# Passing the first four blocks of a gated feed-forward network in two halves of its inner columns, and splitting half of its weights later

## Chip, core and metric

The kernel runs on one core of a Trainium2 chip. The metric is device time in microseconds (us) of one execution. The engines are named as the profile names them: PE is TensorE (PEld its weight load), DVE is VectorE, ACT is ScalarE, POOL is GpSimd, SP is SyncE, which issues most DMAs.

## The reference

All values are float32. Three stages follow one another on the same 3072 tokens (4 batches of 768) of width 320.

```python
# 1 recurrence: 4 x 8 heads, 768 steps, state 40 x 40
y[t] = r[t] @ state
state = state*w[t] - outer(state @ a[t], b[t]) + outer(v[t], k[t])
# 2 eight experts, one per token (D = 320, F = 1024)
logits = x @ w_gate + modality_bias[modality_id];  e = argmax(logits)
out[e_idx==e] = softmax(logits)[e] * (relu(x[e_idx==e] @ w1[e]) @ w2[e])
# 3 gated network, 3072 tokens (D = 320, inner F = 1536)
g = x @ w_gate2;  out = (silu(g) * (x @ w_val)) @ w_out
```

## The kernel before

The recurrence fills the first 570 us and is not touched. What follows is one function, `main`, whose instructions are issued in the order in which the code is written; every engine takes its own in that order.

**Precision.** A float32 matrix is used as two parts, a rounded one ("h") and the remainder ("l"); a product is three matmuls, h·h, l·h and h·l (`mm3`, L607 to L610). The last 64 of the 320 rows carry h and l in one tile, so a column of 128 inner units takes eight matmuls (`up`). An activation is split where it arises: ACT writes the rounded part, DVE the remainder.

**Experts.** The tokens, sorted by expert, fill eight static slots: seven of 384 tokens, slot 1 of 512. Each slot takes four steps `p` of 256 inner columns: up-matmuls, ReLU and split (`evac`, tile `hl`, L926), down-matmuls (tile `pd`). Each step also splits the next weights: ACT casts (L663), POOL subtracts (L664), two POOL instructions a step. The results go to a buffer `y1` in DRAM.

**Second network's weights.** Its three matrices come as the float64 numbers of the input, and are made into h and l parts on the chip by 22 chunks of eight operations each (`split64`, L566 to L576), eight on DVE with two beside them on ACT. That is 176 operations, taken one by one from a generator. A chunk is (gate, c), (value, c) of 192 inner columns or (out, c) of 256 inner rows, c rising. `prepare` takes them during slots 1 to 7 at an even rate: 150 of 176 by the last expert step, the rest in the first block of the second network.

**Second network.** The tokens pass in nine blocks, of 2, 3, 3, 3, 3, 3, 3, 2 and 2 tiles of 128. A block takes twelve columns `fc` of 128 inner units: up for gate and for value, silu on ACT (L1075), product on DVE (L1077, here "mul"), cast on ACT (L1080), remainder on DVE (L1081), and the down-matmuls one column later (`down2`). After column 11 the sums are copied to `ys` (L1058) and stored or scattered by POOL (L1059). The tokens of the next block are gathered by POOL from `y1` at column 0 (`xload`, L962), their gates at column 4 (`gates`, L967 and L968), multiplied on DVE at columns 7 to 9 (`gmul`, L972), and transposed on PE and split at columns 8 to 10 (`xt2`, L647, L622 to L624).

Buffers that matter: `pu` for the up-products has two, gate and value of one column; `pd` has four of one tile; `xg` has four; the split tokens `X` have two sets, for even and odd blocks.

Of the kernel before, what the change touches and what calls it, by code (L numbers as in the profile page):

```python
# [492 lines left out]
Q = {'SK': 8.0, 'TL': 11.0, 'RP': 12, 'ORD': '1dD2bBx', 'F2': (0, 4, 7), 'RS': [1, 4, 5, 3, 0, 3, 1, 2, 0, 0, 0, 0, 0, 0, 0, 0, 0, 0, 0, 0, 0, 0, 0, 0], 'G6': 0, 'HV': 1, 'DP': (1,), 'NV': 1, 'V1': (3,), 'V2': (2,)}  # L493
# [117 lines left out]
def up(T,out,w,x,fs,between=None):  # L611


    wh,wl=w; xh,xl=x
# [3 lines left out]
    T.matmul(out,wh[:,2,fs],xh[:,2],start=False,stop=False)  # L618
    T.matmul(out,wl[:,2,fs],xh[:,2],start=False,stop=True)  # L619
def xsplit(nc,ps,xh,xl,ts):  # L620
    V,A=nc.vector,nc.scalar
    A.copy(xh[:,0:2,ts],ps[:,0:2]); A.copy(xh[0:64,2,ts],ps[0:64,2])  # L622
    V.tensor_tensor(xl[:,0:2,ts],ps[:,0:2],xh[:,0:2,ts].bitcast(F32),ALU.subtract)
    V.tensor_tensor(xh[64:128,2,ts],ps[0:64,2],xh[0:64,2,ts].bitcast(F32),ALU.subtract)  # L624
class Moe:
# [13 lines left out]
    def xalloc(s, j):  # L639
        return tuple(s.xp.tile([128,3 if x=="xh" else 2,128*tiles(j%2)],F32R,tag=x+"eo"[j%2],name=x)[:,:,0:128*tiles(j)] for x in ("xh","xl"))  # L640
# [246 lines left out]
    def main(s, LG, y1, gd, wg, wv, wo, out):  # L887
        tc=s.tc; nc=s.nc; V,A,G,T=nc.vector,nc.scalar,nc.gpsimd,nc.tensor; C=s.C
        s.gd=gd
        with ExitStack() as ctx:  # L890
# [64 lines left out]
            XG={}; ID={}; GT={}  # L955
# [7 lines left out]
            def gates(b):  # L963
                if b>=len(blocks) or blocks[b][0]<0: return
                n=len(blocks[b])
                ID[b]=P.tile([128,NT,2],I32,tag="id",bufs=3,name="id"); GT[b]=P.tile([128,NT],F32,tag="gt",bufs=2,name="gt")
# [10 lines left out]
            def cut(x,n): return tuple(y[:,:,0:n] for y in x)  # L977
            def loop(n):
# [71 lines left out]
            def down2():  # L1050
                b,fc,hh,hl=pn; n=len(blocks[b])
                if fc==0: pds[b]=pdt(n)
                pd=pds[b]
                down(pd,fc==0,fc==11,hh,hl,W["o"][0][:,fc],W["o"][1][:,fc])
                if fc<11: return
                ys=ystile(); lastb=b==len(blocks)-1
# [110 lines left out]
```

## Time and profile before

| | us |
|---|---|
| median of 3 runs (1232.97 to 1238.61) | 1236.4 |
| profiled execution, its own time | 1238.5 |
| its span, first to last instruction | 1236.8 |
| PE busy over the span | 1073.2 (87%) |
| DVE busy | 853.8 (69%) |
| ACT, POOL busy | 557.7, 553.2 |
| mean granted TensorE clock | 0.938 |

The span has three parts: the recurrence to about 570 us, the experts to about 826 us, the second network to the end. A share over the whole span mixes them, so each part is read by itself.

### The profile page before, as it was taken

To read this page: it belongs to the slowest core of one execution; us is meant where nothing else is said; L and a number is where in the kernel's file an instruction comes from. 1 tells how busy PE (TensorE), PEld (TensorE's weight loads), DVE (VectorE), ACT (ScalarE), POOL (GpSimd) and SP (SyncE) were. 2 spreads that over 40 slices of the span, in tenths; PEclk is the share of its full clock that TensorE was granted. 3 is DMA by queue.
4 is the path that set the end of the run, shared out by engine and by line. 5 is a ranking of instruction groups with operands and counts; after the bars stand their busy time and mean duration, and the time that the engine had idled before them with its cause. 6 is when DMAs were issued, how large, how long until landed. Compare 5 with 4: busy or idle time off the path is not lost.

```text
span 1236.8 us, 27832 instructions
## 1 busy us (share of the span) xinstructions
PE 1073.2 (87%) x10437; PEld 1010.8 (82%) x10437; DVE 853.8 (69%) x1979; ACT 557.7 (45%) x1344; POOL 553.2 (45%) x1068
## 2 busy tenths in 40 slices
PE   5367888889889987987897787889999999999998
PEld 4356777778778877877787787889999999999998
DVE  5998898988888988645699999997233332333332
ACT  5355567566666664452354444443222222222232
POOL 7885676676656766221556556523111112111000
PEclk9677999999998899887998988899999999999999
DMA  6544446654555434312566566532000000000000
GB/s 108 88 78 86 79 74 114 118 118 87 99 105 98 79 78 87 83 47 73 157 185 177 164 186 185 156 106 72 17 22 21 18 17 23 28 11 28 11 17 12
DMA packets 278321, 102.39 MB, mean 83 GB/s; under 512 B 235713, under 2 KB 272961, under 8 KB 278177
## 3 DMA queue, kind: packets, MB, share of 16 engines
q1 hardware_dynamic: 270864, 85.56, 31.2%
q0 software_dynamic: 3856, 11.02, 3.0%
q10 hardware_dynamic: 3456, 3.93, 0.9%
q8 instruction: 86, 1.41, 0.5%
q14 instruction: 59, 0.48, 0.1%
HBM read 77.56 MB, written 22.90 MB: 81 GB/s over the span
## 4 chain that ended last, share of the span: by engine, by line
PE 36%; DVE 9%; issue 3%; DMA 1%; POOL 1%; ACT 1%; SPq 1%; DVEq 0%; POOLq 0%; ACTq 0%
PE pu L608 6%; PE pu L609 6%; PE pu L610 6%; PE pd L609 4%; PE pd L608 4%; PE pd L610 4%; PE pu L618 3%; PE pu L619 3%; DVE cva L575 1%; DVE cvm L569 1%; DVE hl L926 1%; DVE cva L567 1%; DVE cva L571 1%; DVE cva L568 1%; PE xt L647 1%
## 5 line engine op out<-in xcount | busy, mean ns | idle before, releaser
L1077 DVE TENSOR_TENSOR s<-s,pu 128x384 f32<-128x384 f32 (+1 forms) x108 | 55.0, 509 | 183.0 <-PE pu L619 180.3
L664 POOL TENSOR_TENSOR l<-s,h 128x768 fp32r<-128x768 f32 (+1 forms) x62 | 117.4, 1909 | 130.0 <-ACT h L663 118.4
L266 POOL TENSOR_TENSOR tmp<-Lb,Pm 128x60 f32<-128x60 f32 (+22 forms) x348 | 107.9, 310 | 54.3 <-DMA Lb<-LD 28.3
L266 DVE TENSOR_TENSOR tmp<-Lb,Pm 128x60 f32<-128x60 f32 (+24 forms) x372 | 112.0, 301 | 19.5 <-DMA Lb<-LD 8.3
L1080 ACT CAST hh<-s 128x384 fp32r<-128x384 f32 (+1 forms) x108 | 51.6, 478 | 146.9 <-DVE s L1077 146.8
L269 DVE TENSOR_TENSOR Pm<-Pm,tmp 128x60 f32<-128x60 f32 (+24 forms) x372 | 109.4, 294 | 9.4
L269 POOL TENSOR_TENSOR Pm<-Pm,tmp 128x60 f32<-128x60 f32 (+22 forms) x348 | 102.3, 294 | 26.6 <-POOL tmp L266 0.3
L1075 ACT ACTIVATE s<-pu 128x384 f32<-128x384 f32 (+1 forms) x108 | 49.1, 455 | 122.6 <-PE pu L619 122.6
L1081 DVE TENSOR_TENSOR hl<-s,hh 128x384 fp32r<-128x384 f32 (+1 forms) x108 | 55.5, 514 | 58.3 <-ACT hh L1080 58.3
L609 PE MATMUL pd<-woh,hl 128*128 128x320 f32 x288 | 89.1, 309 | 0.0
L608 PE MATMUL pd<-woh,hh 128*128 128x320 f32 x288 | 88.8, 308 | 0.1
L610 PE MATMUL pd<-wol,hh 128*128 128x320 f32 x288 | 88.8, 308 | 0.0
L608 PE MATMUL pu<-xh,h 128*128 128x384 f32 (+1 forms) x128 | 52.7, 411 | 40.0 <-DVE hl L926 32.8
L1059 POOL DMA_INDIRECT out_dram<-ys,id x20 | 19.7, 987 | 145.6 <-DVE ys L1058 115.5
L198 POOL TENSOR_TENSOR ks<-I,rawb 64x320 f32<-64x320 f32 x48 | 49.4, 1029 | 51.6 <-DVE I L194 23.9
L608 PE MATMUL pu<-xh,wgh 128*128 128x384 f32 (+1 forms) x216 | 70.7, 327 | 1.1 <-ACT s L1075 0.9
L608 PE MATMUL pu<-xh,wvh 128*128 128x384 f32 (+1 forms) x216 | 68.6, 318 | 0.1
L609 PE MATMUL pu<-xh,wgl 128*128 128x384 f32 (+1 forms) x216 | 68.6, 318 | 0.0
L610 PE MATMUL pu<-xl,wvh 128*128 128x384 f32 (+1 forms) x216 | 68.4, 317 | 0.0
L609 PE MATMUL pu<-xh,wvl 128*128 128x384 f32 (+1 forms) x216 | 68.4, 317 | 0.0
L610 PE MATMUL pu<-xl,wgh 128*128 128x384 f32 (+1 forms) x216 | 68.3, 316 | 0.0
L608 PEld LDWEIGHTS pu<-xh,h 128*128 128x128 f32 x128 | 28.0, 219 | 45.5 <-DVE hl L926 37.4
(338 smaller groups left out, 3407.4 us busy)
## 6 DMA issues: line engine op xcount, KB each, us to landing
s<-in_moe_w_dram SPq DMA_DIRECT2D x32, 320.0 KB, 3.4
s<-in_moe_w_dram SPq DMA_DIRECT2D x32, 256.0 KB, 2.9
Lb<-LD SPq DMA_DIRECT2D x24, 256.0 KB, 3.9
s<-in_moe_w_dram SPq DMA_DIRECT2D x64, 64.0 KB, 2.9
y<-zrow SPq DMA_DIRECT2D x8, 483.0 KB, 4.3
raww<-in_w_dram SPq DMA_DIRECT2D x24, 160.0 KB, 3.3
rawa<-in_a_dram SPq DMA_DIRECT2D x24, 160.0 KB, 3.6
rawk<-in_k_dram SPq DMA_DIRECT2D x24, 160.0 KB, 2.9
```

What stands on the lines that cost most here:

```text
L198: EN('ksb').tensor_tensor(KS[64:128,cc],I0[s],R["b"][s],ALU.mult)
L266: E.tensor_tensor(tmp[:,0:k_,0:ni],Lb[:,j+1:32,j].unsqueeze(1).to_broadcast([128,k_,ni]), Pm[:,0:k_,j].unsqueeze(2).to_broadcast([128,k_,n ...
L269: E.tensor_tensor(Pm[:,0:k_,j+1:32],Pm[:,0:k_,j+1:32],tmp[:,0:k_,0:ni],ALU.add)
L608: T.matmul(out,lh,rh,start=first,stop=False)
L609: T.matmul(out,ll,rh,start=False,stop=False)
L610: T.matmul(out,lh,rl,start=False,stop=last)
L618: T.matmul(out,wh[:,2,fs],xh[:,2],start=False,stop=False)
L664: (E or s.nc.gpsimd).tensor_tensor(hl[1][:],t[:],hl[0][:].bitcast(F32),ALU.subtract)
L1075: A.activation(sg,pg,AF.Silu)
L1077: V.tensor_tensor(sg,sg,pv,ALU.mult)
L1080: A.copy(hh,sg)
L1081: V.tensor_tensor(hl,sg,hh.bitcast(F32),ALU.subtract)
```

## The change

The first four blocks (`HB`: 4) go through the second network twice: first blocks 0 to 3 with inner columns 0 to 5 each, then blocks 0 to 3 with columns 6 to 11, and only then the other five blocks with all twelve. The sums of a first half are kept in SBUF (`partials`, tile `yp`, in buffers that the experts no longer use) and added on DVE after the second half (L1078 of the changed kernel). So four sets of split tokens live at once; those of blocks 2 and 3 lie in the experts' weight buffers (`xspare`), and the 64-row part is a tile of its own (`x2`).

The 176 operations are paced anew: 96 (`W1`) spread over the slots, the other 80 over the 24 columns of the first halves. In the first halves the next block is only six columns away, so its gather is at six columns ahead, its gates at four, the multiplication at three and the transposes at two and one ("near").

```diff
-Q = {'SK': 8.0, 'TL': 11.0, 'RP': 12, ... 'F2': (0, 4, 7), ...}
+Q = {'SK': 8.0, 'RP': 12, 'W1': 96, 'HB': 4, ...}
             def prepare(f):
-                k=f-Q['SK']
-                while k>=0 and done*(2*NP-Q['SK']-1+Q['TL'])<nbetween*(k+1):
+                while done<nbetween and done<need(f):
                     g=next(between,None); done+=1
                     if g: g()
+            def need(f):
+                k=f-Q['SK']; n=2*NP-Q['SK']
+                return Q['W1']*(k+1)/n if f<2*NP else Q['W1']+(nbetween-Q['W1'])*(f-2*NP+1)/(6*HB-1)
+            passes=[(b,0) for b in range(HB)]+[(b,1) for b in range(HB)]+[(b,2) for b in range(HB,len(blocks))]
-                if i==0: X['b',b]=s.xalloc(NSTAT+b)
+                if i==0: X['b',b]=s.xspare(b) if 2<=b<HB else s.xalloc(NSTAT+b)
+                if h==0: YP[b]=partials(b)
+                else: ys=ystile()
+                for i,t in enumerate(blocks[b]):
+                    if h==1: V.tensor_tensor(ys[:,i,0:320],pd[i][:,0:320],YP[b][i],ALU.add)
+                    else: (A.copy if i%2 else V.tensor_copy)(YP[b][i] if h==0 else ys[:,i,0:320],pd[i][:,0:320])
+                near=start[b]-start[b-1]<12
+                at=[start[b]-x for x in ((6,4,3) if near else (12,8,5))]
+                    todo2.setdefault(at[2]+i,[]).append(lambda b=b,i=i: gmul(b,i))
+                    todo2.setdefault(at[2]+i+(not near or i<2),[]).append(lambda b=b,i=i: xt2(b,i))
-            for b in range(len(blocks)):
-                for fc in range(12):
+            for b,h in passes:
+                for fc in ((0,1,2,3,4,5),(6,7,8,9,10,11),range(12))[h]:
-                    if b==0:
-                        prepare(2*NP+fc)
                     ...
                     V.tensor_tensor(hl,sg,hh.bitcast(F32),ALU.subtract)
                     if pn: down2()
+                    prepare(2*NP+k)
+                    for f in todo2.get(k,()): f()
+                    k+=1
```

DVE at the passage from the last expert step to the second network, before; L567 to L576 are the eight operations of a chunk, L926 the experts' remainder, L1077 and L1081 the network's mul and remainder, L935 and L937 the experts' last store copies:

```order
L926 SCALAR_TENSOR_TENSOR hl<-pu,hh 128x384 x2
L567 TENSOR_SCALAR cva<-st_12087 128x576
L568 SCALAR_TENSOR_TENSOR cva<-st_12087,cva 128x576
L569 TENSOR_SCALAR cvm<-st_12087 128x576
L571 SCALAR_TENSOR_TENSOR cva<-cvu,cva 128x576
L573 TENSOR_SCALAR cvu<-cva 128x576
L574 SCALAR_TENSOR_TENSOR cvm<-cvm,cvu 128x576
L575 TENSOR_TENSOR cva<-cva,wgh 128x576
L576 SCALAR_TENSOR_TENSOR wgl<-cvm,cva 128x3x192
L1077 TENSOR_TENSOR s_12215<-s_12215,pu 128x256
L935 COPY ys<-kslot 128x3x2
L937 COPY ys<-pd 128x320
```

The same place now; lines have moved, so that L931, L940 and L942 are the experts' remainder and copies, and L1111 and L1115 the network's mul and remainder:

```order
L931 SCALAR_TENSOR_TENSOR hl<-pu,hh 128x384 x2
L574 SCALAR_TENSOR_TENSOR cvm<-cvm,cvu 128x640
L575 TENSOR_TENSOR cva<-cva,woh 128x640
L576 SCALAR_TENSOR_TENSOR wol<-cvm,cva 128x640
L1111 TENSOR_TENSOR s_12111<-s_12111,pu 128x256
L940 COPY ys<-kslot 128x3x2
L942 COPY ys<-pd 128x320
L1115 TENSOR_TENSOR hl<-s_12111,hh 128x256
L567 TENSOR_SCALAR cva<-st_12054 128x576
L568 SCALAR_TENSOR_TENSOR cva<-st_12054,cva 128x576
L569 TENSOR_SCALAR cvm<-st_12054 128x576
L571 SCALAR_TENSOR_TENSOR cva<-cvu,cva 128x576
```

Before the last expert remainder stand 144 operations of the splitting before the change and 93 now; before the first mul 152 and 96. The rest follows the columns in threes and fours.

DVE at the end of block 0 before the change, its columns 9 to 11 and the first of block 1 (L972 gmul, L623 and L624 the two remainders of the split tokens):

```order
L1077 TENSOR_TENSOR s_12589<-s_12589,pu 128x256
L1081 TENSOR_TENSOR hl<-s_12589,hh 128x256
L972 TENSOR_SCALAR xg<-xg,gt 128x320
L623 TENSOR_TENSOR xl<-xt,xh 128x2x128
L624 TENSOR_TENSOR xh<-xt,xh 64x128
L1077 TENSOR_TENSOR s_12631<-s_12631,pu 128x256
L1081 TENSOR_TENSOR hl<-s_12631,hh 128x256
L623 TENSOR_TENSOR xl<-xt,xh 128x2x128
L624 TENSOR_TENSOR xh<-xt,xh 64x128
L1077 TENSOR_TENSOR s_12670<-s_12670,pu 128x256
L1081 TENSOR_TENSOR hl<-s_12670,hh 128x256
L1077 TENSOR_TENSOR s_12701<-s_12701,pu 128x384
```

DVE at the end of block 0's first half now, its column 5 and the first of block 1 (L983 is gmul):

```order
L1111 TENSOR_TENSOR s_12353<-s_12353,pu 128x256
L1115 TENSOR_TENSOR hl<-s_12353,hh 128x256
L569 TENSOR_SCALAR cvm<-st2o 128x640
L571 SCALAR_TENSOR_TENSOR cva<-cvu,cva 128x640
L573 TENSOR_SCALAR cvu<-cva 128x640
L623 TENSOR_TENSOR xl<-xt,xh 128x2x128
L624 TENSOR_TENSOR x_12341<-xt,x_12341 64x128
L983 TENSOR_SCALAR xg<-xg,gt 128x320
L623 TENSOR_TENSOR xl<-xt,xh 128x2x128
L624 TENSOR_TENSOR x_12341<-xt,x_12341 64x128
L1111 TENSOR_TENSOR s_12409<-s_12409,pu 128x384
L1115 TENSOR_TENSOR hl<-s_12409,hh 128x384
```

The last tile of the next block is now multiplied and split behind the last remainder of the block, with nothing between it and the next block's first mul; before, a whole column lay between them.

## Rows read from the trace of the kernel before

**Rows 1.** The page's 40 slices of the span; busy tenths.

```profile
PE   5367888889889987987897787889999999999998
...
DVE  5998898988888988645699999997233332333332
```

**Rows 2.** Busy us of each engine, sum of 608 to 826 (us).

```profile
sum 218.00, PE 183.74 PEld 176.05 DVE 208.08 ACT 101.39 POOL 120.94; mean PE 22.97 PEld 22.01 DVE 26.01 ACT 12.67 POOL 15.12
```

**Rows 3.** Waits, 608 to 826: total us, times, longest.

```profile
PE pu L608 <- DVE hl L926: 30.9, 15, 4.7
```

**Rows 4.** Timeline of DVE in an expert slot: start, duration, instruction.

```profile
740.77 2.15 DVE L575 TENSOR_TENSOR cva<-cva,wvh 128x576 f32<-128x576 f32 x1
...
747.03 2.04 DVE L568 SCALAR_TENSOR_TENSOR cva<-st2o,cva 128x640 int32<-128x640 int32 x1
```

**Rows 5.** Timeline of POOL at the same place.

```profile
740.44 7.94 POOL L664 TENSOR_TENSOR l<-s,h 128x768 fp32r<-128x768 f32 x4 [3.26 <-ACT h L663]
```

**Rows 6.** Timeline of PE in an expert slot, first instructions of each run.

```profile
740.02 0.42 PE L608 MATMUL pu<-xh,h 128*128 128x384 f32 x1
...
742.89 0.31 PE L608 MATMUL pd<-h,hh 128*128 128x320 f32 x1
...
745.53 0.49 PE L647 MATMUL xt<-ident,xg 128*128 128x128 f32 x3
750.74 0.69 PE L608 MATMUL pu<-xh,h 128*128 128x384 f32 x1 [4.72 <-DVE hl L926]
...
754.74 0.42 PE L609 MATMUL pu<-xh,l 128*128 128x384 f32 x1
```

**Rows 7.** Timeline of PE from the second network's first matmul.

```profile
826.17 0.38 PE L608 MATMUL pu<-xh,wgh 128*128 128x256 f32 x1
...
830.66 0.31 PE L610 MATMUL pd<-l,hh 128*128 128x320 f32 x1
...
840.03 0.28 PE L608 MATMUL pu<-xh,wgh 128*128 128x256 f32 x1
...
842.73 0.28 PE L608 MATMUL pu<-xh,wgh 128*128 128x256 f32 x1
...
1014.61 0.33 PE L608 MATMUL pu<-xh,wgh 128*128 128x384 f32 x1
```

**Rows 8.** Timeline of DVE in the second network's first block.

```profile
826.50 0.45 DVE L567 TENSOR_SCALAR cva<-st 128x576 int32<-128x576 int32 x1
...
831.44 0.41 DVE L1077 TENSOR_TENSOR s<-s,pu 128x256 f32<-128x256 f32 x1
...
834.20 0.42 DVE L1077 TENSOR_TENSOR s<-s,pu 128x256 f32<-128x256 f32 x1
...
835.43 0.75 DVE L571 SCALAR_TENSOR_TENSOR cva<-cvu,cva 128x576 f32<-128x576 f32 x1
...
837.39 0.41 DVE L1077 TENSOR_TENSOR s<-s,pu 128x256 f32<-128x256 f32 x1
...
856.42 0.38 DVE L972 TENSOR_SCALAR xg<-xg,gt 128x320 f32<-128x320 f32 x1
...
857.44 0.76 DVE L575 TENSOR_TENSOR cva<-cva,wvh 128x576 f32<-128x576 f32 x1
```

**Rows 9.** Timeline of DVE in a block of three tiles, and one pair of store copies.

```profile
871.16 0.55 DVE L1077 TENSOR_TENSOR s<-s,pu 128x384 f32<-128x384 f32 x1 [1.60 <-PE pu L619]
872.30 0.56 DVE L1081 TENSOR_TENSOR hl<-s,hh 128x384 fp32r<-128x384 f32 x1 [0.58 <-ACT hh L1080]
875.27 0.55 DVE L1077 TENSOR_TENSOR s<-s,pu 128x384 f32<-128x384 f32 x1 [2.42 <-PE pu L619]
...
919.24 0.88 DVE L1058 COPY ys<-pd 128x320 f32<-128x320 f32 x2
```

**Rows 10.** Timeline of POOL: the first gather of block 1.

```profile
837.83 0.96 POOL L962 DMA_INDIRECT xg<-y,krank  x1 [15.84 <-DMA y<-ys]
```

**Rows 11.** DMA issues: kind, count, median us to landing.

```profile
xg<-y,krank POOLq DMA_INDIRECT x18, 3.0
```

More of the change, by code (lines that the diff above doesn't have):

```diff
@@ L639, in xalloc, with xspare @@
     def xalloc(s, j):
-        return tuple(s.xp.tile([128,3 if x=="xh" else 2,128*tiles(j%2)],F32R,tag=x+"eo"[j%2],name=x)[:,:,0:128*tiles(j)] for x in ("xh","xl"))
+        n=128*tiles(j)
+        return tuple(s.xp.tile([128,*k,128*tiles(j%2)],F32R,tag=x+"eo"[j%2],name=x)[...,0:n] for x,k in (("xh",[2]),("xl",[2]),("x2",[])))
+    def xspare(s, b):
+        h,l=(t[:].rearrange("p a b -> p (a b)").rearrange("p (k n) -> p k n",k=2) for t in s.h1tiles(b))
+        return h,l,(s.wp[1].tile([128,512],F32R,tag="scr",name="x2s") if b==2 else s.wp[1].tile([128,SL],F32R,name="x2t"))[:,0:SL]
     def xg(s):
@@ L974, in xt2, with cut, partials @@
                 if b>=len(blocks) or i>=len(blocks[b]): return
-                if i==0: X['b',b]=s.xalloc(NSTAT+b)
+                if i==0: X['b',b]=s.xspare(b) if 2<=b<HB else s.xalloc(NSTAT+b)
                 s.xtile(X['b',b],XG[b][i],i,px())
-            def cut(x,n): return tuple(y[:,:,0:n] for y in x)
+            def cut(x,n): return tuple(y[...,0:n] for y in x)
+            def partials(b):
+                l=[]
+                for i in range(len(blocks[b])):
+                    k=sum(map(len,blocks[:b]))+i
+                    if k%2==0: YT.append(s.wp[k//2%2].tile([128,2,320],F32,tag=("h2","l2","s2")[k//4],name="yp"))
+                    l.append(YT[k//2][:,k%2])
+                return l
             def loop(n):
@@ L1050, in down2 @@
             def down2():
[L1051 to L1052 removed]
+                b,h,fc,hh,hl=pn; n=len(blocks[b]); f0,f1=((0,5),(6,11),(0,11))[h]
+                if fc==f0: pds[b]=pdt(n)
                 pd=pds[b]
[L1054 to L1060 removed]
@@ new lines, in down2 @@
+                del pds[b]
+            start={}; k=0
+            for b,h in passes:
+                if h!=1: start[b]=k
+                k+=6 if h<2 else 12
+            todo2={}
+            for b in range(1,len(blocks)):
+                near=start[b]-start[b-1]<12
+                at=[start[b]-x for x in ((6,4,3) if near else (12,8,5))]
+                todo2.setdefault(at[0],[]).append(lambda b=b: xload(b))
+                todo2.setdefault(at[1],[]).append(lambda b=b: gates(b))
+                for i in range(NT):
+                    todo2.setdefault(at[2]+i,[]).append(lambda b=b,i=i: gmul(b,i))
+                    todo2.setdefault(at[2]+i+(not near or i<2),[]).append(lambda b=b,i=i: xt2(b,i))
@@ L1067, in main @@
                     sg=s.w1tile()[:].rearrange("p a b -> p (a b)")[:,0:n]
-                    if b==0:
-                        prepare(2*NP+fc)
-                        need=8*(((128*fc+127)//192*11+3)//4)+16 if 0 else 8*NEED[fc]
-                        while done<need and done<nbetween:
-                            f=next(between,None); done+=1
-                            if f: f()
+                    while done<8*NEED[fc] and done<nbetween:
+                        f=next(between,None); done+=1
+                        if f: f()
                     up(T,pg,W["g"],x,fs)
```

42 lines of the change are left out of this document (21 added, 21 removed).

## The prediction

> **What bounds the kernel now.** I read the 40 slices first. In the experts' part, slices 21 to 27, DVE shows nine tenths in nearly every slice; behind it DVE falls to three tenths and PE stands at nine to the end [rows 1]. So the two parts have different bounds, and the change moves work of the first one's bound into the second, where that engine is two thirds idle.
>
> Then the busy sums from step 4 (the first with splitting, 608 us) to the second network's first matmul at 826.17. Of these 218 us DVE is busy 208, PE 184, POOL 121 [rows 2]. The waits say who is late: PE stood 30.9 us before up-matmuls until DVE had written a remainder [rows 3]. These are 28 steps, so one takes 218/28 = 7.8 us. PE's own work in a step of 384 tokens is the up-matmuls from 740.02 to 742.89, the downs to 745.53 and transposes of a quarter us, 5.76 in all; by columns the 512-token steps come to 7.6 [rows 6]. PE alone would need 24 x 5.76 + 4 x 7.6 = 169 us.
>
> Last the timelines, for what DVE does in 7.8 us. While POOL runs four subtractions back to back (7.94 us), DVE gets through exactly four operations, the first at 740.77 and the last ending at 749.07: two us each [rows 4, 5]. The same kind without POOL beside it takes 0.62 us: the eight of a chunk from 826.50 to 831.44 are 4.94 [rows 8]. So a step is two operations at POOL's pace (4.1 us), three and a third at 0.62 (2.1), and the remainders and copies: 7.8.
>
> The Trainium skill (SBUF — State Buffer, "Who interferes with whom") says that a DVE instruction with two SBUF inputs and a GpSimd instruction that reads SBUF exclude each other, and that the second to issue blocks until the first is done; rows 4 and 5 agree. By that rule the hold belongs to the POOL instruction: 56 stay, so thinning DVE's work would return 0.62 an operation and not two us.
>
> **The change, part by part.**
>
> Experts. Before the last expert remainder stand 93 operations of the splitting in place of 144 (the listing with the change). 51 fewer at 0.62 are 32 us, the lower end. POOL's own work is as before, so the two operations a step at POOL's pace stay. The upper end is PE's 169, a gain of 49. One step falls to 7.8 - 1.15 = 6.6 us, still over PE's 5.76: DVE remains the bound, so I stay near the lower end and allow 4 us for POOL instructions that now meet DVE at a remainder read from PSUM. Gain 36. The two ACT operations per chunk and the loads of the weights lie off DVE's path and go with them. PE's shorter waits also spare it slow restarts, which are inside these ends.
>
> Second network, before. From 826.17 to the first matmul of block 4 at 1014.61 it takes 188.4 us [rows 7].
>
> First halves, now. 80 operations fall on 24 columns, 3.5 a column. In block 0 mul to end of remainder is 1.23 us (834.20 to 835.43), three operations follow, and the next mul comes at 837.39: DVE sets the pace there against PE's 2.70 a column [rows 7, 8]. In a three-tile block mul to end of remainder is 1.70, a column on PE 4.11 [rows 9]; with 3.5 x 0.62 DVE has 3.9, so alone it would still hide. But each first half also carries the next block: gmul and two remainders, 1.02 us a tile from 856.42 to 857.44 [rows 8]. And the last tile's come behind all other work of the last column, with the next block's first mul right after them: PE cannot start the block before them, and DVE has nothing to do until PE's first two up-products exist. In the kernel before a whole column lay between.
>
> Block 0, on DVE's path from 826.17: PE's last expert downs end at 830.97, 4.8 us in [rows 7]; store copy, cast and remainder, some 0.45 each (as the copies and casts of rows 8 and 9), bring the first remainder to 6.1. Then 21 operations at 0.62 (13.0), five columns at 1.23 (6.2), three tiles at 1.02 (3.1), and for the last tile 0.5 of transposes [rows 6] and as much again on ACT, by estimate: 1.0. Together 29.4. The gather stood until the last experts' store had landed (837.83) [rows 10]; the three stores now issue 1 to 2 us earlier. With three issues of about 1 us and 3.0 to land [rows 11] its tokens come 15 to 17 us in, DVE asks for them at 16; I add 0.5. So 29.9.
>
> Blocks 1 and 2, each: PE's first up pair 2.9 [rows 6], six columns at 1.70 (10.2), 21 operations (13.0), three tiles (3.1), store copies and index copies (1.0) [rows 9], the last tile's 1.0: 31.2, where PE would take 24.7. Twice: 62.4. Block 3 has no near successor, its surplus hides: 6 x 4.11 = 24.7.
>
> Second halves: nothing is left to split, PE holds the pace. 6 x 2.70 + 18 x 4.11 = 90.2; the additions in place of copies lie beside PE. With 0.8 of block 4's transposes the path is 29.9 + 62.4 + 24.7 + 90.2 + 0.8 = 208.0, which is 19.6 more than before.
>
> Restarts. After 4.72 us of idleness PE's next matmuls came 0.32 us apart instead of 0.17, the lower clock; from 750.74 to 754.74 that cost about 1.8 us [rows 6]. At the starts of blocks 1, 2 and 3 PE will have waited 5 to 8 us, and DVE waits for these very products: up to 3 x 1.8 = 5.4. I take 4. Cost 24.
>
> Its ends: if the operations all hide and only the three serial starts remain (2.9 + 1.0 each), 12. If besides the 25 each near block's gates arrive late (fetched one column ahead instead of three: three one-column gathers of about 1 us and 3.0 to land, against a column of 3.5 to 4.5, so up to 2 us) and DVE's mul waits behind ACT's cast of a chunk (up to 1 us, three times), 34.
>
> Sum. 1238.5 - 36 + 24 = 1226.5 for an execution like the profiled one, which lay 2.1 above the median; against the median 1224.4. I say 1224.
>
> **Rivals.**
>
> *The hold goes too.* With a lighter DVE, POOL could more often find it idle or at PSUM, so that the slots fall to PE's 169: 1236.4 - 49 + 24 = 1211. For it: POOL is busy 121 of 218, so half the time there is no hold. Against: its instructions follow the casts right when DVE begins its splitting [rows 4, 5].
>
> *Given back.* Gain at its lower end, 32, and the first halves near their upper, 32: 1236. The gathers are the weak place, and the margins there are below 2 us.
>
> *PE slows in the first halves.* There PE works some 25 of 31 us and waits in every block. If the granted clock falls to 1.2 GHz and stays there until block 3, a three-tile column takes twice 4.11 and blocks 1 and 2 last 50 us each, 19 more apiece, block 0 about 3: 1236.4 - 36 + 20 + 41 = 1261, slower. It decides as soon as PE at half clock is slower than DVE, 8.2 against 5.2 a column. Against: after 4.72 us of idleness the low rate lasted 4 us and ended under work as dense as this [rows 6]. The Trainium skill (TensorE: Matmul & The Clock Gate, "What's actually happening") calls the throttled state the default that activity releases; a stage with gaps everywhere is where that rule would bring this rival about.
>
> *It does not thin the slots.* If loads of weights, not DVE, set the slots, nothing is gained and the halves cost 24: 1260. DVE's 208 of 218 speaks against it.
>
> **How the numbers follow.** A measurement of this kernel tells about 0.5% (6.2 us) from no change. Forecast 0.55 (1224, own range 1214 to 1236), hold gone 0.20, given back 0.13, PE slow 0.08, slots not thinned 0.04. Below 1230 lie the hold gone and four fifths of the forecast: 0.64. Within 0.5% lie the given-back case and the rest of the forecast: 0.24. Slower keeps 0.12. The range leaves out the two slow rivals and the lower end of the hold's case: 1207 to 1240.
>
> **What would show it.** Experts: 4 to 12 DVE operations of two us fewer and the stretch from step 4 to the second network at about 182 us, DVE still over nine tenths; at 170 with PE full, the hold went too. Second network: the first halves of blocks 0, 1 and 2 about 30, 31 and 31 us long plus a slow restart each, PE waiting at the start of blocks 1, 2 and 3 for a remainder of split tokens and nowhere else for long; second halves at 16 and 25 us with PE unbroken. Wrong is the account if blocks 1 and 2 take 25 us (the work hides), if their matmuls run at 0.32 us apart throughout (the clock), or if DVE waits for gathers.

## The result and the profile after

The changed kernel takes 1246.2 us (median of 5 runs, 1245.3 to 1249.5) against 1236.4 for the kernel before: ratio 1.0089, 95% interval 1.0067 to 1.0112. It is slower by about 10 us, where the forecast was 12 faster. The profiled execution took 1248.84 us, with a span of 1247.1.

Two stretches carry nearly all of it. "Slots" runs from the first 512-token up-matmul of step 4 to the second network's first matmul, "path" from there to block 4's first matmul:

| | slots | first halves of blocks 0, 1, 2, 3 | second halves | path |
|---|---|---|---|---|
| before | 218.2 | (whole blocks: 38.2, 49.8, 50.0, 50.3) | | 188.4 |
| forecast | 182 | 29.9, 31.2, 31.2, 24.7, and 4 of restarts | 91.0 | 212.0 |
| after | 195.6 | 32.5, 33.8, 34.5, 26.6 | 91.8 | 219.2 |

So the slots gave 22.6 us where 36 were taken, and the path cost 30.8 where 24 were. The slots of one kernel differ by up to 4 us between profiled executions: in the six kernels here whose slots are the same (after, e3, e4, e6, e7 and e8) they took 192.4 to 196.8, 194.6 in the mean.

The page's slices after, to be held against [rows 1]; the columns are 40 equal parts of the span:

```profile
PE   5367899889888888987898898868899999999998
...
DVE  5998798988888987636699999867763343333332
```

DVE still shows nines in slices 21 to 25, so it stays the bound of the slots. Slices 27 to 30 are the first halves: DVE has 6, 7, 7, 6 there, and PE, at nine from slice 28 on before, only 6, 8, 8 in slices 27 to 29. Neither engine is full, so they wait for each other.

The slots after, in one window (busy us of PE, PEld, DVE, ACT and POOL, each with its number of instructions, then the granted clock and two DMA columns; answers to [rows 2]), under it the same of the kernel before, and then the waits of DVE and PE in the slots after (total, times, longest; [rows 3]), with DVE's wait in the kernel before under them:

```profile
609.20:804.80 195.60, 175.28 (x1027) 168.62 (x1028) 178.14 (x229) 95.49 (x189) 119.09 (x72) 0.96 0.56 165
```

```profile
608.00:826.20 218.20, 183.82 (x1028) 176.08 (x1028) 208.28 (x278) 101.39 (x201) 120.94 (x72) 0.91 0.56 167
```

```profile
DVE hl L931 <- ACT hh L930: 12.5, 6, 6.8
DVE xl L623 <- ACT x L622: 4.7, 5, 1.2
...
PE pu L608 <- DVE hl L931: 11.3, 8, 2.8
```

```profile
DVE hl L926 <- ACT hh L925: 8.7, 5, 6.9
```

DVE's busy time fell from 208 to 178 us, 30 us for 51 operations. But it now stands idle 17.5 us of the stretch in place of 10, waiting for ACT: new is the wait at the split of tokens (L623), which before had none, and 3.8 us more at the remainder (its longest, 6.8 and 6.9, opens the stretch in both). 30.1 less 7.5 is the 22.6. One of the new waits, on DVE and then on ACT:

```profile
720.35 0.75 DVE L571 SCALAR_TENSOR_TENSOR cva<-cvu,cva 128x576 f32<-128x576 f32 x1
722.27 0.42 DVE L623 TENSOR_TENSOR xl<-xt,xh 128x256 fp32r<-128x256 f32 x1 [1.17 <-ACT x L622]
```

```profile
721.14 0.67 ACT L572 CAST wgh<-cva 128x576 fp32r<-128x576 f32 x1 [3.98 <-DVE cva L571]
721.72 0.37 ACT L622 CAST xh<-xt 128x256 fp32r<-128x256 f32 x1
721.98 0.26 ACT L622 CAST x<-xt 64x128 fp32r<-64x128 f32 x1
```

L571 is the fourth of a chunk's eight operations, and the step's share of splitting (the operations that `prepare` takes in one step) ends on it. ACT's cast of that chunk (L572) then stands ahead of its cast of the tokens, and DVE has nothing left to do in between. In the changed kernel's trace a token split waits 1.17 us each time the share before it ended on the fourth operation (three times), 0.46 or 0.69 us where it ended on the fifth (twice), and not at all elsewhere; remainders that follow such a share directly wait in the same way (1.13 us behind a fourth, 0.66 at one of two behind a fifth). Together these are 6.5 of the 7.5 us. Before, the even rate of 16 operations in three steps ended every share on the third, sixth or eighth operation.

What became of the hold? The same groups of splitting operations in the slots before, after, and with POOL's subtraction moved to DVE (e9 below); columns: count, busy us and mean ns of one, idle time before them (us):

```profile
L574 DVE SCALAR_TENSOR_TENSOR cvm<-cvm,cvu 128x576 f32<-128x576 f32 (+1 forms) x18 | 17.6, 978 | 0.6
...
L568 DVE SCALAR_TENSOR_TENSOR cva<-st,cva 128x576 int32<-128x576 int32 x12 | 16.5, 1375 | 0.4
```

```profile
L574 DVE SCALAR_TENSOR_TENSOR cvm<-cvm,cvu 128x576 f32<-128x576 f32 (+1 forms) x12 | 22.7, 1896 | 0.3
L568 DVE SCALAR_TENSOR_TENSOR cva<-st,cva 128x576 int32<-128x576 int32 x8 | 20.5, 2560 | 0.2
```

```profile
L664 DVE TENSOR_TENSOR l<-s,h 128x640 fp32r<-128x640 f32 (+1 forms) x53 | 45.4, 883 | 1.0 <-ACT h L663 0.9
...
L574 DVE SCALAR_TENSOR_TENSOR cvm<-cvm,cvu 128x576 f32<-128x576 f32 (+1 forms) x18 | 14.1, 781 | 0.6
...
L568 DVE SCALAR_TENSOR_TENSOR cva<-st,cva 128x576 int32<-128x576 int32 x12 | 9.1, 758 | 0.4
```

Over all fifteen such groups the sums are 159.8 us for 144 operations before, 126.0 for 95 after, and 95.3 for 144 without POOL, 0.66 each. So the hold (what is over 0.66 an operation) was 64.5 us before and is 63.3 after. It did not shrink with the operations: it only fell on fewer of them, and L568 went from 1.4 to 2.6 us each. This is the rule of the Trainium skill that the prediction weighed, by which the two engines exclude each other (SBUF — State Buffer, "Who interferes with whom"), and the trace agrees: the hold is POOL's, 53 subtractions in both kernels.

The start of block 1 after, on PE (answers to [rows 7]), then on DVE and on ACT; start, duration, instruction, idle time before it:

```profile
835.91 0.87 PE L652 MATMUL xt<-ident,xg 128*128 128x128 f32 x3 [4.21 <-issue]
837.25 0.69 PE L608 MATMUL pu<-xh,wgh 128*128 128x384 f32 x1 [0.46 <-ACT xh L622]
837.74 0.52 PE L609 MATMUL pu<-xh,wgl 128*128 128x384 f32 x1
...
840.93 0.52 PE L608 MATMUL pu<-xh,wvh 128*128 128x384 f32 x1
841.25 0.43 PE L609 MATMUL pu<-xh,wvl 128*128 128x384 f32 x1
841.52 0.34 PE L610 MATMUL pu<-xl,wvh 128*128 128x384 f32 x1
```

```profile
832.23 0.48 DVE L569 TENSOR_SCALAR cvm<-st2o 128x640 int32<-128x640 int32 x1
832.63 0.82 DVE L571 SCALAR_TENSOR_TENSOR cva<-cvu,cva 128x640 f32<-128x640 f32 x1
833.49 0.49 DVE L573 TENSOR_SCALAR cvu<-cva 128x640 int32<-128x640 int32 x1
834.67 0.42 DVE L623 TENSOR_TENSOR xl<-xt,xh 128x256 fp32r<-128x256 f32 x1 [0.69 <-ACT x L622]
835.11 0.28 DVE L624 TENSOR_TENSOR x<-xt,x 64x128 fp32r<-64x128 f32 x1
835.43 0.39 DVE L983 TENSOR_SCALAR xg<-xg,gt 128x320 f32<-128x320 f32 x1
837.38 0.42 DVE L623 TENSOR_TENSOR xl<-xt,xh 128x256 fp32r<-128x256 f32 x1 [1.57 <-ACT x L622]
837.84 0.28 DVE L624 TENSOR_TENSOR x<-xt,x 64x128 fp32r<-64x128 f32 x1
842.32 0.56 DVE L1111 TENSOR_TENSOR s<-s,pu 128x384 f32<-128x384 f32 x1 [4.20 <-PE pu L619]
```

```profile
833.48 0.73 ACT L572 CAST woh<-cva 128x640 fp32r<-128x640 f32 x1 [1.63 <-DVE cva L571]
834.12 0.37 ACT L622 CAST xh<-xt 128x256 fp32r<-128x256 f32 x1
834.38 0.26 ACT L622 CAST x<-xt 64x128 fp32r<-64x128 f32 x1
836.82 0.37 ACT L622 CAST xh<-xt 128x256 fp32r<-128x256 f32 x1 [2.18 <-PE xt L652]
```

PE takes its instructions in order. The next in its line is the last three transposes of block 1 (L652), and they need the gated tokens (L983), which DVE writes only at 835.43, behind three splitting operations and behind a wait for ACT, whose cast of a weight chunk (L572) stands ahead of the token cast. PE stood 4.2 us. Then ACT casts the tokens (836.82), and PE starts at 837.25; DVE's remainder, which PE's third matmul reads, comes beside it at 837.38. The granted clock of 837.25 to 841.25 is 0.50, the lower of the two levels: the matmuls come 0.32 us apart until 841.25, then 0.18. DVE in turn has no work until 842.32. The same came at blocks 2 and 3. PE's largest wait over all first halves:

```profile
PE xt L652 <- issue: 17.6, 7, 4.2
```

### The profile page after: what moved, and what is told of

Read it like the earlier page. It is cut to its first block, busy times and chain, and to the rows that moved or that the text cites. A ratio compares the mean times of both kernels' runs of the same rounds, so it can differ in the third digit from the quotient of the medians.

```text
span 1247.1 us, 27834 instructions
## 1 busy us (share of the span) xinstructions
PE 1078.9 (87%) x10437; PEld 1015.0 (81%) x10437; DVE 857.7 (69%) x1990; ACT 560.8 (45%) x1344; POOL 551.9 (44%) x1068
## 4 chain that ended last, share of the span: by engine, by line
PE 40%; DVE 5%; issue 3%; DMA 1%; POOL 1%; ACT 1%; SPq 0%; DVEq 0%; ACTq 0%; POOLq 0%
PE pu L608 7%; PE pu L609 6%; PE pu L610 6%; PE pd L609 4%; PE pd L608 4%; PE pd L610 4%; PE pu L618 3%; PE pu L619 3%; PE xt L652 1%; DVE hl L931 1%; DMA s<-in_moe_w_dram 1%; POOL l L669 1%; DVE cva L575 0%; DVE cvu L573 0%; DVE cvm L574 0%
## 5 line engine op out<-in xcount | busy, mean ns | idle before, releaser
L1111 DVE TENSOR_TENSOR s<-s,pu 128x384 f32<-128x384 f32 (+1 forms) x108 | 55.0, 509 | 167.5 <-PE pu L619 164.3
L669 POOL TENSOR_TENSOR l<-s,h 128x768 fp32r<-128x768 f32 (+1 forms) x62 | 113.5, 1847 | 112.1 <-ACT h L668 95.3
L1081 POOL DMA_INDIRECT out_dram<-ys,id x20 | 19.8, 989 | 234.9 <-DVE ys L1078 103.4
L1115 DVE TENSOR_TENSOR hl<-s,hh 128x384 fp32r<-128x384 f32 (+1 forms) x108 | 55.6, 515 | 59.6 <-ACT hh L1114 59.1
L608 PE MATMUL pu<-xh,h 128*128 128x384 f32 (+1 forms) x128 | 49.9, 390 | 25.3 <-DVE hl L931 13.2
L609 PE MATMUL pd<-h,hl 128*128 128x320 f32 x200 | 62.0, 310 | 1.3 <-DVE hl L931 1.3
L668 ACT CAST h<-s 128x640 fp32r<-128x640 f32 (+1 forms) x64 | 49.8, 781 | 28.6 <-issue 17.3
L608 PE MATMUL pd<-h,hh 128*128 128x320 f32 x200 | 62.2, 311 | 0.0
L610 PE MATMUL pd<-l,hh 128*128 128x320 f32 x200 | 61.9, 310 | 0.0
L374 PE MATMUL pq<-rbd,VT 128*128 128x128 f32 x384 | 60.3, 308 | 0.0
L316 PE MATMUL zz<-pbd,MA 128*104 128x128 f32 x384 | 56.9, 299 | 3.2 <-ACT pbd L138 1.1
L223 PE MATMUL sc<-kbt,atb 128*128 128x128 f32 x384 | 54.0, 295 | 3.7 <-ACT atb L209 2.9
```

Of the source, the lines that this page charges most:

```text
L223: T.matmul(ps[:,q].rearrange("p s j -> p (s j)"),ATB[0][:,4*c+q].rearrange("p s j -> p (s j)"),X[i,c][:,q],start=True,stop=True)
L316: T.matmul(ps[0:104,h],u['MA'][:,8*i+4*g+h,0:104],pbd[:,4*g+h],start=True,stop=True)
L374: T.matmul(pq[:,q],X['VT',c][:,q],RBD[0][:,q,cc].rearrange("p s t -> p (s t)"),start=True,stop=True)
L608: T.matmul(out,lh,rh,start=first,stop=False)
L609: T.matmul(out,ll,rh,start=False,stop=False)
L610: T.matmul(out,lh,rl,start=False,stop=last)
```

## The experiments

The kernel of before ran beside each; every ratio is to it. Slots and path are those of the one profiled execution.

| run | slots | path | median us | ratio (95%) |
|---|---|---|---|---|
| e1_w150 | 221.5 | 206.2 | 1255.8 | 1.0177 (1.0126 to 1.0227) |
| e3_whole | 196.8 | 229.5 | 1254.3 | 1.0164 (1.0119 to 1.0209) |
| e4_early | 192.4 | 217.6 | 1245.4 | 1.0099 (1.0060 to 1.0137) |
| e6_swap | 195.7 | 211.5 | 1240.3 | 1.0025 (1.0000 to 1.0051) |
| e7_apart | 193.7 | 215.0 | 1238.9 | 1.0012 (0.9991 to 1.0034) |
| e8_ahead | 193.6 | 206.0 | 1230.9 | 0.9950 (0.9924 to 0.9975) |
| e10_ahead150 | 221.6 | 193.0 | 1248.6 | 1.0083 (1.0051 to 1.0116) |
| e12_w64 | 177.1 | 239.0 | 1246.9 (one run) | |
| e13_pair | 194.1 | 218.9 | 1244.5 | 1.0075 (1.0041 to 1.0110) |
| e15_thin | 196.1 | 215.8 | 1240.2 | 1.0048 (1.0021 to 1.0075) |
| e16_thin150 | 224.7 | 206.2 | 1261.9 | 1.0215 (1.0157 to 1.0274) |
| e5_nohold | 167.5 | 217.8 | 1213.8 | 0.9839 (0.9807 to 0.9872) |
| e9_dve | 192.0 | 188.3 | 1209.1 | 0.9781 (0.9763 to 0.9799) |
| e17_plain | 172.1 | 217.1 | 1218.5 | 0.9884 (0.9836 to 0.9932) |
| e11_both | 172.4 | 204.5 | 1206.8 | 0.9757 (0.9702 to 0.9811) |
| e14_w120 | 180.5 | 197.7 | 1210.6 | 0.9800 (0.9767 to 0.9833) |

### One part of the change alone

e1_w150 keeps the halves, but leaves nearly all splitting in the slots.

```diff
-Q = {... 'W1': 96 ...}
+Q = {... 'W1': 150 ...}
```

> The halves alone: the changed kernel with 150 of the 176 splitting operations in the slots, as before the change, and 26 in the first halves. Theory A (each near block starts behind its own last tile, and DVE is overloaded on top of that): slots 218 us again; the path from the first matmul of the second network to block 4, 188 before and 220 in the changed kernel, comes to about 199, because three serial starts of some 4 us remain when the load is gone; 1247 us. Rival B (the cost is the load of 80 operations alone): about 190, 1238 us.

e3_whole thins the slots, but passes the blocks whole, with 80 operations in block 0.

```diff
-Q = {... 'HB': 4 ...}
+Q = {... 'HB': 0 ...}
-... (f-2*NP+1)/(6*HB-1)
+... (f-2*NP+1)/(6*HB-1 if HB else 11)
```

> The new rate alone: 96 operations in the slots and the other 80 in the twelve columns of block 0, no halves (all nine blocks in one pass). Theory A: the slots' time hangs on their own load, so they take 196 us as in the changed kernel (218 before); block 0 then takes 6.1 + 11 x (1.25 + 6.7 x 0.62) + 4 = 70 us in place of 38, so that about 1245 us come out. Rival B (the slots became shorter by something else in the changed kernel, such as the buffers): slots 205 or more, 1255 us.

Neither half of the change pays alone. The slots follow the operations in them, whatever comes after: 221.5 with 150, 196.8 with 96. The halves with only 26 operations still cost 17.8 us of path (206.2 against 188.4; 199 was expected), so more than half of the path's loss does not come from the operations moved. And 80 operations in one block cost 41 us (block 0 took 79.1 where 70 was expected), in four first halves 31: the halves do hide some, though little.

e1 also shows that the new waits in the slots do not need fewer operations. It has 150 there, as before, and its token splits wait all the same, after shares that the changed pacing ends on the fourth operation:

```profile
DVE xl L623 <- ACT x L622: 3.6, 3, 1.2
```

### The second network: where the late starts come from

e4_early gathers, gates and transposes the tokens of blocks 2 and 3 one column earlier; gating and transposes stay in one column.

```diff
-at=[start[b]-x for x in ((6,4,3) if near else (12,8,5))]
+at=[start[b]-x for x in (((6,4,3) if b==1 else (7,5,4)) if near else (12,8,5))]
```

> The changed kernel with the preparation of blocks 2 and 3 one column earlier (gather seven ahead, gates five, multiplication four, transposes three and two), so that a whole column lies between the last tile and the block's first mul, as before the change. Theory A (serial starts): the first halves of blocks 1 and 2 fall from 34 us to about 29 each and 1246 to 1236 us. Rival B (DVE's operations set the pace, wherever they stand): no more than 1 us each, 1244 us.

A miss: the path stayed (217.6, and blocks 1 and 2 at 35.1 and 33.8). PE only stood at the transposes one column sooner (4.64 us at 858.42): the wait is for the multiplication just ahead in DVE's queue, not for the block's start.

e6_swap issues the column's gating and transposes ahead of its splitting operations; e7_apart instead puts the last tile's multiplication one column ahead of its transposes.

```diff
-                    prepare(2*NP+k)
                     for f in todo2.get(k,()): f()
+                    prepare(2*NP+k)
```

> The changed kernel with one order swapped in each column of the second network: the next block's multiplication, transposes and token split stand ahead of the column's three or four splitting operations, not behind them. Theory A (PE takes its instructions in order and stands at the next block's last transposes, because the multiplication they read is queued on DVE behind the splitting): PE's waits of 4.2 us at the transposes fall to about 1.5 and the first halves of blocks 0 to 2 from 32, 34 and 34.5 us to about 30, 31 and 31; 1237 us. Rival B (DVE's total work sets these passes, in whatever order): no more than 1 us a pass, 1244 us.

```diff
-todo2.setdefault(at[2]+i,[]).append(lambda b=b,i=i: gmul(b,i))
+todo2.setdefault(at[2]+(min(i,1) if near else i),[]).append(lambda b=b,i=i: gmul(b,i))
```

> The changed kernel with the third tile's multiplication one column earlier, so that it no longer stands in the same column as its transposes; nothing else moves. Theory A: PE no longer waits for it, but the tile's split still ends the last column, so only the transposes and the ACT cast leave the series: 1.5 us at each of three starts, 1242 us. Rival B: nothing, 1246 us.

Each gave part: 7.7 and 4.2 us of path. e8_ahead does all three: earlier for blocks 2 and 3 (now by two columns), transposes a column behind the multiplication, splitting last.

```diff
-at=... ((6,4,3) if near else (12,8,5))
+at=... (((6,4,3) if b==1 else (8,6,5)) if near else (12,8,5))
-todo2.setdefault(at[2]+i,[]).append(lambda b=b,i=i: gmul(b,i))
-todo2.setdefault(at[2]+i+(not near or i<2),[]).append(lambda b=b,i=i: xt2(b,i))
+todo2.setdefault(at[2]+(min(i,1) if b==1 else i),[]).append(lambda b=b,i=i: gmul(b,i))
+todo2.setdefault(at[2]+(min(i,1) if b==1 else i)+1,[]).append(lambda b=b,i=i: xt2(b,i))
-                    prepare(2*NP+k)
                     for f in todo2.get(k,()): f()
+                    prepare(2*NP+k)
```

> Both of these (the swap, and the multiplication a column ahead of the transposes), and for blocks 2 and 3 the preparation two columns earlier (gather eight ahead, gates six, multiplication five to three, transposes four to two), so that the last column carries none of it. Theory A: blocks 1 and 2 come down to the larger of PE's 25 us and DVE's 27, and block 0 to 30; the path to block 4 from 219 to about 203 us; 1230 us. Rival B: first halves of 33 us as before, since the splitting alone fills DVE; 1244 us.

e10_ahead150 is the same with a window of 150.

```diff
-Q = {... 'W1': 96 ...}
+Q = {... 'W1': 150 ...}
```

> The kernel of e8 (next block prepared ahead) with 150 operations in the slots, as before the change, and 26 in the first halves: the fourth corner of a square whose paths to block 4 are 219 us (80 operations, prepared late), 206 (26, late) and 206 (80, ahead), against 188 before. Theory A (late starts and DVE's load are two costs of 13 us that add up): 193 us, slots 219, 1240 us. Rival B (they are one cost, in which each hides behind the other): 204 us, 1252 us.

With these the path is known at four corners: 219.2 (80 operations, late), 206.2 (26, late), 206.0 (80, ahead), 193.0 (26, ahead). The late starts cost 13 us and the 54 operations cost 13 us, whether the other is there or not; 4.6 us over the 188.4 remain. The first halves in one window each of the changed kernel, e8 and e10, and then PE's two largest waits in e8's:

```profile
804.80:932.20 127.40, 105.96 (x620) 101.88 (x619) 85.56 (x172) 40.83 (x91) 18.52 (x18) 0.91 0.20 59
```

```profile
800.40:914.70 114.30, 102.98 (x620) 100.08 (x619) 85.88 (x172) 40.36 (x91) 19.27 (x18) 0.94 0.22 66
```

```profile
831.20:932.40 101.20, 97.29 (x621) 96.36 (x620) 54.27 (x119) 34.40 (x79) 18.32 (x18) 0.98 0.11 32
```

```profile
PE pu L608 <- ACT s L1109: 6.8, 7, 1.8
PE pu L608 <- ACT xh L622: 3.6, 1, 3.6
```

DVE is busy 86 us in both of the first two, and the wait at L652 is no longer among PE's waits in e8. Of the 13.1 us that e8 took away, 10.1 are idle time of PE and 3.0 busy time, for the same 620 matmuls. Of the 13.1 from e8 to e10, 7.4 are idle time and 5.7 busy time. PE's granted clock rises 0.91, 0.94, 0.98 with its shorter gaps. e8 is the first version of the change that is faster than before, by half a percent.

### The slots: what an operation moved is worth

e12_w64 moves 32 more operations out.

```diff
-Q = {... 'W1': 96 ...}
+Q = {... 'W1': 64 ...}
```

> The changed kernel with 64 operations in the slots in place of 96 (the rest in the first halves, which grow); only the slots are read. Theory A (per step the later of PE and DVE decides, so each further operation taken out is worth less): 194 to 187 us, 0.2 us an operation. Rival B (DVE is the bound throughout, each operation at 0.62 and more): 194 - 20 = 174 us.

The slots fell 17.5 us from that mean of six at 96 (194.6), 0.55 us an operation; from 150 to 96 (e1 to that mean) it was 26.9 for 54, 0.50. So no diminishing return shows down to 64, against my theory A of then (the spread of 4 us between slots is some 0.1 in either price). But the path rose by 20, and the sum stayed.

Next, DVE's new waits for ACT. In the changed kernel a group of one or two splitting operations can end on the fourth of a chunk, whose cast on ACT then stands ahead of the cast that DVE needs. In e13_pair no group ends there.

```diff
-while done<nbetween and done<need(f):
+while done<nbetween and (done<need(f) or done%8==4):
```

> The changed kernel; a group of splitting operations never ends on the last operation of a chunk. Theory A (in the slots VectorE waits for ScalarE because the cast behind a chunk's last operation stands ahead of the cast that VectorE needs next): VectorE's extra waits at L623 and L931 go, some 8 us, the slots take 187 to 189 us in place of 195, the first halves' columns lose about 1 us each, and the kernel takes some 1237 us. Rival B (the waits for ScalarE lie beside VectorE's hold and cost nothing, or come from another cast): the slots stay at 193 to 196 us and the time at 1246.

```profile
DVE hl L931 <- ACT hh L930: 11.8, 6, 6.4
DVE xl L623 <- ACT x L622: 3.2, 5, 0.7
DVE ys L942 <- PE pd L610: 1.8, 2, 1.0
```

The waits at L623 shrank (4.7 to 3.2 us, the longest 1.2 to 0.7), and the slots took 194.1, inside the spread of the six. Theory A had the wait right and the remedy wrong: the three splits that stood behind a fourth operation now stand behind a fifth and wait 0.67 us in place of 1.17, so of the 8 us that were to go only some 2 went, too little to be told from the spread, and another wait grew (L942, 0.3 to 1.8). What these waits cost the slots is therefore not shown by a run. e15_thin makes TensorE's work in the slots lighter: from the second slot on, and for all but the first token tile, it leaves out the product of the rounded hidden values with the low part of the weights (the expectation names another of the three products; the work saved is the same). e16_thin150 has the same edit and a window of 150.

```diff
-def down(pd,first,last,hh,hl,wh,wl):
+def down(pd,first,last,hh,hl,wh,wl,thin=False):
 for i in range(len(pd)):
     ts=slice(128*i,128*i+128)
+    if i and thin:
+        T.matmul(pd[i][:,0:320],hh[:,ts],wh,start=first,stop=False)
+        T.matmul(pd[i][:,0:320],hl[:,ts],wh,start=False,stop=last)
+        continue
     mm3(T,pd[i][:,0:320],hh[:,ts],hl[:,ts],wh,wl,first,last)
 ...
-down(PD[j],fc==0,fc==7,hh,hl,w2h[:,q],w2l[:,q])
+down(PD[j],fc==0,fc==7,hh,hl,w2h[:,q],w2l[:,q],j>=1)
```

> The changed kernel; in the experts' slots from the second on, the third product of the second layer (low part of the hidden values by the high weights) is left out for all but the first token tile, so TensorE has some 15 to 20 us less to do there and VectorE as much as before. Theory C (a step takes the longer of TensorE's and VectorE's work, and where TensorE is later VectorE stands, which the next step doesn't give back): with TensorE's work thinner VectorE is the later one almost everywhere, its idle time falls from some 17 us to about 9 (what was idle before the change), and the slots take 186 to 189 us in place of 195. Rival D (VectorE's idle time comes from a fixed way through ScalarE or from the order of the casts): idle time stays at 16 to 18 us and the slots at 193 to 196.

```diff
-Q = {... 'W1': 96 ...}
+Q = {... 'W1': 150 ...}
```

> As the run beside it, with a window of 150 in place of 96, so that the slots hold nearly as many splitting operations as before the change. Theory C: VectorE is the later engine here anyway, the slots stay at 218 to 222 us, and against the run beside it the 54 operations moved are worth 32 to 36 us of slots (27 with TensorE's whole work), so that the time is some 18 us over that run's. Rival D: 25 to 28 us of slots, and a time some 10 us over that run's.

```profile
DVE hl L931 <- ACT hh L930: 14.5, 9, 5.9
DVE xl L623 <- ACT x L622: 4.6, 5, 1.2
...
PE pu L608 <- DVE hl L931: 27.0, 13, 5.1
```

The fence shows e15. DVE's idle time stayed (14.5 and 4.6) and the slots too (196.1), while PE waited 27.0 us for remainders in place of 11.3. Its thinner work went into waiting, not into the end, so theory C (PE later in some steps) has this trace against it. The token splits wait as in the changed kernel (1.2 us behind a fourth operation, 0.5 and 0.7 behind a fifth), which is D's order of the casts. The times seem to speak for C: e16 lies 21.7 us above e15, where C had 18 and D 10. But between the two profiled executions (21.3) the slots make 28.6 us, which is next to D's 28 and short of C's 32, though the spread of the slots reaches both; the path gives back 9.6, where D had reckoned with more, and 2.3 lie ahead of the slots. So the idle time speaks for D, and the times decide nothing.

### The hold itself

e5_nohold lets POOL write zeros in place of the subtraction from step 4 on, so that these instructions no longer read SBUF; the low parts of those weights are left out. `late` is the number of the step.

```diff
-(E or s.nc.gpsimd).tensor_tensor(hl[1][:],t[:],hl[0][:].bitcast(F32),ALU.subtract)
+if E or s.late<4: (E or s.nc.gpsimd).tensor_tensor(hl[1][:],t[:],hl[0][:].bitcast(F32),ALU.subtract)
+else: s.nc.gpsimd.memset(hl[1][:].bitcast(F32),0.0)
 ...
```

> The changed kernel with POOL's subtraction of the experts' weights replaced by a POOL memset from step 4 on, so the low parts of those weights are left out. Theory A (POOL's reading instructions hold DVE up, and the slots are late by that): splitting operations fall from 1.30 us on average to about 0.65 in the slots, and the slots from 196 to about 172 us; 1222 us in all. Rival B (the slots are now set by PE and the loads of weights, with DVE late only now and then): slots 190 us or more, 1241 us.

e9_dve is the kernel of before, with the subtraction on DVE in all steps from 2 on.

```diff
-Q = {... 'V1': (3,), 'V2': (2,) ...}
+Q = {... 'V1': tuple(range(3,32)), 'V2': tuple(range(2,32)) ...}
```

> The kernel before the change with one thing moved: the subtraction that makes the low parts of the experts' weights is done by DVE in place of POOL in all steps from 2 on. Theory A (each POOL subtraction holds DVE up for about 1.3 us, as much as DVE needs to do it itself, 1.30 and 0.82 us for the two tiles): a step is 7.8 - 2.6 + 2.1 = 7.3 us, the slots 205 instead of 218 us, 1223 us. Rival B (POOL's work runs beside DVE's, and DVE is late by its own operations): 2.1 us are added to each of 28 steps, 1295 us.

Without the hold the changed kernel's slots are 167.5, with PE busy 167.47 of them: this is PE's own pace, which the prediction had put at 169. In e9 DVE does 45.4 us more (L664, shown above), gets 64.5 us of hold back on the splitting operations alone, and its busy time falls from 208.3 to 181.9. The kernel is 2.2% faster with nothing else touched, twice the 13 us expected; a subtraction takes DVE 0.88 us in the mean, where 1.30 and 0.82 had been put for the two tiles:

```profile
604.80:796.80 192.00, 171.73 (x1028) 162.95 (x1029) 181.85 (x331) 100.50 (x201) 19.61 (x19) 0.99 0.64 189
```

e17_plain is the changed kernel and e11_both is e8 with that same edit.

```diff
-Q = {... 'V1': (3,), 'V2': (2,) ...}
+Q = {... 'V1': tuple(range(3,32)), 'V2': tuple(range(2,32)) ...}
```

> The changed kernel with the subtraction that splits the experts' weights on VectorE in place of GpSimd, the order of the second network as in the changed kernel. The two gains don't add up if the slots are then bound by TensorE: slots 177 us, path to the fifth block 219, so about 1226 us, some 17 us over the kernel of before with the same edit (1209). If they did add up: 1246 less 27, 1219.

> The kernel of e8 with the subtraction of the experts' weights on DVE, as in e9. Theory A (without the hold the slots have nothing to gain but the distance from 192 us to PE's own 177, and the halves still cost 18): 1209 - 15 + 18 = 1212 us, so that the change is worth nothing once the hold is gone. Rival B (moving operations out of the slots still pays 0.42 us each, 54 of them): 1209 - 23 + 18 = 1204 us.

```profile
602.60:774.70 172.10, 169.41 (x1028) 163.83 (x1029) 150.94 (x282) 94.65 (x189) 21.03 (x19) 0.99 0.63 186
```

The window is e17's. e17 lies 9.4 us over e9: its slots are 20 us shorter and its path 29 longer. DVE again lost 31 us of work for 51 operations (181.85 to 150.94), but the slots only 20, since PE is now busy 169 of 172: there it is the bound. The expectation had PE bound the slots at 177 and the gains not add up; at 172.1 they nearly do (46.1 us of slots, where the change alone gave 22.6 and e9 alone 26.2), and 1218.5 is the time named for that case. e11 has both repairs, and its median is the lowest of all, between the 1212 and the 1204 expected; its interval overlaps e9's, so that which of the two is better is not settled.

e14_w120 is e11 with the pacing of e13 and a window of 120.

```diff
-Q = {... 'W1': 96 ...}
+Q = {... 'W1': 120 ...}
-while done<nbetween and done<need(f):
+while done<nbetween and (done<need(f) or done%8==4):
```

> The kernel with VectorE subtracting (as in the run that had both, 1206.8), with the pacing of the run beside it and a window of 120 in place of 96, so that some 53 operations are left for the second network. If the slots have 3 to 4 us to spare above TensorE's own work, as theory A says, they stay at 177 to 182 us, the first halves lose some 5 us, and the time is about 1203. If each operation in the slots still costs its 0.6 us, the slots take about 186 us and the time is 1208 to 1212.

24 operations back in the slots cost 8.1 us there and spared 6.8 of path: a tie with e11 within the intervals. The slots hit the expected 177 to 182, but not for the reason given: PE's own pace is 167.5, and there was no room for free operations above 172. The time missed the 1203 and fell where each operation still costs its time (1208 to 1212).

## Why the prediction was wrong, point by point

- **What bounds the slots: right.** DVE did, by busy time and waits, and its work fell as the operations left.
- **The hold stays with POOL: right,** 64.5 and 63.3 us. The price of 0.62 us an operation was the measured 0.59 (30.1 for 51). But I did not hold to it and took 36 for the 32 that it gives, for a part of the hold that would be met at reads from PSUM: 6 us too much against the 30.1.
- **"The two ACT operations per chunk and the loads of the weights lie off DVE's path and go with them": the step that failed in the slots.** DVE was taken as busy throughout a step of 6.6 us. In fact 7.5 us of its time turned into waits for ACT, 6.5 of them where a step's share of splitting ends on the fourth or fifth operation of a chunk: ACT's cast of the chunk then stands ahead of the cast that DVE needs next, and no more than one operation of DVE covers it. The new rate moved the ends of the shares there, which the prediction did not look at. The waits are the same 1.2 us in e1 with 150 operations, and e13 moved them from the fourth to the fifth operation and 0.7 us. That the slots would be shorter by these waits follows only from DVE being their bound; no run took them all away.
- **The second network's serial starts: right in place and near in size, with another first wait.** 12 us and 4 of restarts were taken; e8 took 13 away. PE waits there first for the gated tokens, queued on DVE behind splitting, with its own order holding it at the transposes; the prediction had it wait for the remainder of the split tokens and nowhere else for long.
- **DVE's load in the first halves and the restarts: mis-sized, the step that failed in the second network.** Of the 24 us 8 were for the load; e10 took 13 away with 54 of the 80 operations, and 4.6 stay with the other 26. Blocks 0, 1 and 2 took 2.6, 2.6 and 3.3 us more than their sums, which hold no restarts. The restarts were put at 4; PE's busy time for the 620 matmuls is 106.0 us at a mean granted clock of 0.91 and 97.3 in e10 at 0.98, so that the lower clock takes 8.7 us more here than there, and 5.7 of these belong to the 13 of the load. The upper end had named one reason, a mul behind ACT's cast of a chunk, and left it out of the likeliest case; the row below shows one of these waits, after the cast of 850.59. They are a small part: in the changed kernel's first halves they come to 3.2 us, and in e13, with 1.0 us less of them, the path was 218.9. The rest of PE's idle time under the load in e8 is mostly spent until ACT's silu has read `pu` (6.8 us, shown above); what delays ACT there was not tried.

```profile
851.68 0.56 DVE L1111 TENSOR_TENSOR s<-s,pu 128x384 f32<-128x384 f32 x1 [1.13 <-ACT s L1109]
```

- **Block 3 at PE's pace (24.7): nearly,** 26.6. Second halves: 91.0 with 0.8 of transposes, measured 91.8.
- **The rivals.** Given back was nearest in kind, and reality went past it: a gain 9 us below its 32, a cost of 31 where it had 32, and for other reasons than the gathers that it feared: DVE waited for them 0.8 us. The clock did not stay low: at blocks 1 to 3 the matmuls came 0.32 us apart for some 4 us each and then 0.18. The hold did not go by itself.

The sum: -22.6 + 30.8 = +8.2 us by the traces, +9.8 by the medians; of the 10.3 between the profiled spans 1.2 more lie ahead of the slots and 0.9 behind block 4's start. Of the 20 us between the forecast's -12 and this, 13.4 lie in the slots and 6.8 in the second network.

## What to carry to other kernels

When work is taken off the engine that bounds a stage, price it with the hold left out, and look at which operation each portion of the work that stays now ends: if another engine must act on that operation's result, its next service to the bound engine comes late. When a helper engine holds the bound engine, taking away the hold (here 45 us of work for 64 of hold) is worth more than moving work around it. What an engine that takes its instructions in order reads at the head of a block must be ready a column earlier, in a queue that has nothing slow ahead of it (13 us of path here).

## What the runs showed that I had not expected

The subtraction that took POOL 1.9 us takes DVE 0.88 (L664 of e9, 53 of them), so the helper cost more than it carried. POOL's group in the slots of the kernel before:

```profile
L664 POOL TENSOR_TENSOR l<-s,h 128x640 fp32r<-128x640 f32 (+1 forms) x53 | 102.2, 1943 | 85.1 <-ACT h L663 84.5
```
The 4 runs of e9 lie within 0.7 us (1209.0 to 1209.6), against 1228.2 to 1243.0 over the 22 runs of the kernel before beside it. That is not the hold alone: the 4 runs of e17 lie 5 us apart and those of e14 6, with the subtraction on DVE in both. In e5, where POOL's 53 instructions only write zeros, DVE's operations with two inputs take what they take in e9 (L568 on 576 columns 0.75 us against 0.76), while those with one input stay slower (L567 0.62 against 0.46). That POOL's writes hold these is likely, but was not tried by itself. L567 and L568 in e5, then L567 in e9:

```profile
L568 DVE SCALAR_TENSOR_TENSOR cva<-st,cva 128x576 int32<-128x576 int32 x8 | 6.0, 750 | 0.2
...
L567 DVE TENSOR_SCALAR cva<-st 128x576 int32<-128x576 int32 x8 | 4.9, 619 | 0.1
```

```profile
L567 DVE TENSOR_SCALAR cva<-st 128x576 int32<-128x576 int32 x12 | 5.5, 456 | 0.1
```
